# A rebuilt front half of an attention and gMLP block: V and the output projection in 64x128 tiles, weights loaded into both halves, new lists, five half masks and two copies on GpSimd

## The chip, the cores and the metric

The kernel runs on one core of one Trainium2 chip. The metric is device time in microseconds (us). The core has TensorE (PE in the profile, with its weight loads as PEld), VectorE (DVE), ScalarE (ACT), GpSimd (POOL) and SyncE (SP, which here only issues DMAs). Each engine works through its own list in order.

## The reference

Two residual blocks over one sequence of 2048 tokens with 448 features, all inputs in bf16.

```python
S, D, H, Dh, Fh = 2048, 448, 16, 28, 896
# block A: dilated sliding attention, 8 keys at distance 0, 2, ..., 14
qkv = layernorm(x) @ wqkv
logits[s, w] = q[s] . k[s - 2 w] * Dh**-0.5      # masked where s - 2 w < 0
h = x + (softmax(logits) @ v[s - 2 w]) @ wo
# block B: spatial gating
z = gelu(layernorm(h) @ w_in);  z1, z2 = z[:, :Fh], layernorm(z[:, Fh:])
g = w_sp @ z2 + b_sp[:, None]                    # 2048 x 2048 matrix over the tokens
out = h + (z1 * g) @ w_out
```

## The kernel before, in words

The sequence is handled as two halves of 1024 tokens that lie side by side: the features are cut into 7 chunks of 64, and of each chunk the first half's 64 features stand on partitions 0 to 63 and the second half's on 64 to 127 (`xh`). Matmuls with 64 contraction rows then run in pairs, one on each half of the array, into two PSUM banks. For that the weights must be there twice, once in each half of the partitions.

The stages, each named as in the code:

- x is loaded in 16 blocks of 128 tokens (`x0` to `x15`); a unit u is the pair of blocks u and u + 8. Layernorm is statistics (`bn`), aggregate (L819), inverse deviation (`rs`, on GpSimd with L808 and L809, or on ScalarE) and normalization (`nrm`, L838). The result is transposed, for units 0 to 2 of the first layernorm on TensorE (`tT`, L854, then an eviction `ev`), for the others by a DMA transpose on SP's queue (`tD`, L845). The last 16 tokens of the first half are also needed as a halo for the second (`bnh`, `rsh`, `nrmh`, `tTh`, `evh`).
- Q and K (`mmq`, `mmk`, L965) are computed in column chunks, of 128, 128, 256 and 512 tokens of each half, and evicted with L803 (ScalarE) or L805 (VectorE). Their weights are padded from 28 to 32 columns a head, by copies from a staging area (`cpq`, `cpk`).
- Attention runs in 9 tiles of 114 tokens of each half. `mmv` (L1005) makes V for the tile's keys, even and odd tokens apart, in 64x64 tiles of the array: 28 matmuls that read `xh` with a stride of two. `mml` (L1040) makes the logits of all 16 heads, `exp` (L1053) on ScalarE the exponentials, `mask` (L1060) on VectorE multiplies them by a band, `mmr` (L1069) sums them with a matrix of ones, `mmo` (L1089) applies them to V, `ln` and `rex` (L1077, L1099) make the reciprocal of the sums, `ot` (L1107) divides.
- `mmy` (L1143) is the output projection, 8 matmuls of 128x128 a unit: four heads stand on the 128 rows. `h` (L1151) adds x. A second layernorm follows, and z2 (`mmz2`, L1163), Gelu, its layernorm (`bn3`, `rs3`, `nrm3`), z1 (`mmz1`, L1207), the gate (`g`, L1244, 28 groups of 16 matmuls), `ua` and `um` (L1254, L1262), the last projection (`wo0` to `wo15`, L1273), `oa` (L1281) and the store.

The order of the work on each of the five lists is written out by hand in `SEQ`: five tuples of task numbers, for SP, GpSimd, VectorE, ScalarE and TensorE. A task that may run on several engines runs on the one in whose tuple it stands. `replay` walks through the tuples with estimated durations and only hands out buffers with it (PSUM banks, `E`, `V`, `L` and the like); the order itself is the tuples'. Matmuls that only keep TensorE busy can be put in gaps once the task `c_warm` has been placed; before has it at the end of VectorE's tuple, so that there are none.

Of the weights only one copy is loaded, into partitions 0 to 63. wq, wk and wv are loaded on ScalarE's queue (L730). VectorE or ScalarE copies them into the other half: `cpq`, `cpk` (eight copies of 64x1568), `cpv10` (64x3136), `cpw` (four of w_in). The x loads from unit 2 on wait on SP's queue for x8.

## Time and profile before

| | |
|---|---|
| median of 3 runs | 246.23 us (245.85, 246.23, 247.01) |
| span of the profiled execution | 247.4 us, 1.17 above the median of the runs and 0.4 above the slowest |
| TensorE busy | 232.1 us, 94% of the span |
| VectorE, ScalarE, GpSimd busy | 143.3, 91.4, 28.8 us |
| first matmul of Q/K | at 12.38 us |
| first gate matmul of the chain | at 126.57 us |
| last matmul ends | at 244.57 us |

The page lists a time for the profiled execution only as its span, so the span stands for it. A span is counted from the first to the last instruction. The chain of the profile follows the work back from the last instruction: each piece is given with its start, its length and its line; `issue` in it is time for which the profile shows no reason. A matmul's own duration is longer than the time it costs, since matmuls overlap: what a step costs is read from the chain's pieces, not from the mean of its matmuls. PSUM is the matmul's output memory, in eight banks.

### The profile page before, as it was taken

The page shows a single profiled execution, that of the slowest core. Times are in us where ns is not written, and L with a number is a line of the kernel's source. Part 1 is how long each engine was busy: PE and PEld are TensorE (multiplying, and loading weights), DVE is VectorE, ACT ScalarE, POOL GpSimd, SP SyncE. Part 2 cuts the span into 40 slices and gives each one's busy share as a digit, 9 for nine tenths or more (in the row PEclk, how much of TensorE's full clock was granted, in tenths as well). Part 3 has the DMA queues.
Part 4 walks back from the last instruction along what each step waited for, and adds up shares of the span by engine and source line. Part 5 has one row for each costly group of instructions (what it writes and reads, how often), then busy time and mean ns, then how long its engine had stood idle before and what let it go on. Part 6 is the DMA issues. An engine that isn't in the chain of part 4 may idle for free.

```text
span 247.4 us, 6649 instructions
## 1 busy us (share of the span) xinstructions
PE 232.1 (94%) x3004; PEld 123.7 (50%) x3004; DVE 143.3 (58%) x281; ACT 91.4 (37%) x103; POOL 28.8 (12%) x69
## 2 busy tenths in 40 slices
PE   0399799999999999999999999999999999999995
PEld 0297485445556555555544444444444444444442
DVE  6697847779999897798970022335021407541743
ACT  2668784886979965575740000000000000000000
POOL 2843010000021112104530000000000000000000
DMA  6935965893224976886733333100000000010113
GB/s 159 255 80 61 138 91 98 128 154 71 46 40 85 152 197 124 180 147 150 108 85 85 87 85 85 42 3 0 0 0 0 3 0 0 2 46 29 56 57 111
DMA packets 54436, 20.02 MB, mean 81 GB/s; under 512 B 46584, under 2 KB 54280, under 8 KB 54408
## 3 DMA queue, kind: packets, MB, share of 16 engines
q1 hardware_dynamic: 52584, 18.05, 37.4%
q10 hardware_dynamic: 1824, 1.55, 2.8%
q8 instruction: 23, 0.38, 0.7%
q14 instruction: 5, 0.04, 0.1%
HBM read 6.39 MB, written 1.84 MB: 33 GB/s over the span
## 4 chain that ended last, share of the span: by engine, by line
PE 93%; DMA 3%; issue 1%; ACT 1%; ACTq 1%; DVE 0%
PE psum L1244 39%; PE psum L965 11%; PE psum L1163 9%; PE psum L1273 9%; PE psum L1207 9%; PE psum L1005 5%; PE psum L1143 5%; DMA z2p<-in_A_wqkv_dram 3%; PE psum L1040 3%; PE psum L1089 2%; PE psum L1069 1%; ACT reg L803 1%; ACTq L723 1%; ACT xh L803 0%; ACTq L730 0%
## 5 line engine op out<-in xcount | busy, mean ns | idle before, releaser
L1254 DVE TENSOR_TENSOR ub<-psum,reg 128x512 bf16<-128x512 f32 x28 | 18.8, 687 | 64.3 <-PE psum L1244 64.2
L1244 PE MATMUL psum<-reg,z2p 128*128 128x512 bf16 x224 | 50.0, 379 | 0.0
L1244 PE MATMUL psum<-wspT_lo,z2p 128*128 128x512 bf16 x224 | 49.0, 379 | 0.0
L1244 PEld LDWEIGHTS psum<-wspT_lo,z2p 128*128 128x128 bf16 x224 | 21.8, 98 | 26.6 <-issue 0.4
L1244 PEld LDWEIGHTS psum<-reg,z2p 128*128 128x128 bf16 x224 | 21.9, 98 | 26.1
L965 PE MATMUL psum<-xh,reg 64*128 64x128 bf16 (+3 forms) x448 | 28.5, 290 | 2.8 <-issue 2.0
L965 PEld LDWEIGHTS psum<-xh,reg 64*128 64x128 bf16 x448 | 19.4, 105 | 10.5 <-issue 3.4
L1163 PE MATMUL psum<-w_in,xh 64*128 64x448 bf16 x224 | 22.5, 349 | 0.0
L1273 PE MATMUL psum<-reg 128*128 128x448 bf16 x112 | 22.3, 352 | 0.0
L1207 PE MATMUL psum<-xh,w_in 64*128 64x512 bf16 x196 | 22.2, 376 | 0.0
L818 DVE BATCH_NORM_STATS2 st<-x_tm 128x6 f32<-128x448 bf16 x32 | 19.5, 609 | 1.0 <-DMA x_tm<-in_A_x_dram 0.8
L1179 DVE BATCH_NORM_STATS2 st<-z2p 128x6 f32<-128x448 bf16 x32 | 17.7, 612 | 2.6 <-ACT z2p L1173 2.5
L803 ACT ACTIVATE reg<-psum 128x896 bf16<-128x896 f32 (+3 forms) x21 | 16.8, 824 | 5.8 <-PE psum L965 4.2
L1053 ACT ACTIVATE reg<-psum 128x928 bf16<-128x928 f32 x18 | 16.1, 943 | 6.4 <-PE psum L1040 6.4
L1281 DVE TENSOR_TENSOR tring<-psum,x_tm 128x448 bf16<-128x448 f32 x16 | 9.6, 616 | 14.0 <-PE psum L1273 14.0
L808 POOL TENSOR_SCALAR rs<-mv 128x2 f32<-128x2 f32 x21 | 6.3, 300 | 93.7 <-DVE mv L819 78.4
L1173 ACT ACTIVATE z2p<-psum 128x896 bf16<-128x896 f32 x16 | 14.2, 916 | 6.8 <-PE psum L1163 6.8
L1163 PEld LDWEIGHTS psum<-w_in,xh 64*128 64x128 bf16 x224 | 11.9, 94 | 9.5 <-issue 0.9
L1217 ACT ACTIVATE reg<-psum 128x1024 bf16<-128x1024 f32 x14 | 13.7, 1030 | 7.8 <-PE psum L1207 7.8
L1273 PEld LDWEIGHTS psum<-reg 128*128 128x128 bf16 x112 | 11.0, 98 | 10.6
L1207 PEld LDWEIGHTS psum<-xh,w_in 64*128 64x128 bf16 x196 | 11.1, 94 | 9.7
L809 POOL TENSOR_TENSOR rs<-rs,nhalf 128x2 f32<-128x2 f32 x21 | 15.6, 743 | 1.8
(63 smaller groups left out, 201.2 us busy)
## 6 DMA issues: line engine op xcount, KB each, us to landing
out_dram<-tring SPq DMA_DIRECT2D x16, 112.0 KB, 1.7
x_tm<-in_A_x_dram SPq DMA_DIRECT2D x13, 112.0 KB, 5.7
w_in<-in_B_w_in_dram SPq DMA_DIRECT2D x2, 448.0 KB, 5.5
z2p<-in_A_wqkv_dram ACTq DMA_DIRECT2D x2, 392.0 KB, 6.3
reg<-in_B_w_out_dram SPq DMA_DIRECT2D x1, 784.0 KB, 4.8
w_in<-in_B_w_in_dram SPq DMA_DIRECT2D x2, 336.0 KB, 5.1
reg<-in_B_b_sp_dram SPq DMA_DIRECT2D x1, 512.0 KB, 4.2
reg<-in_A_wo_dram SPq DMA_DIRECT2D x4, 98.0 KB
```

What stands on the lines that cost most here:

```text
L803: iss("act", lambda e: e.activation(dst, src, AF.Copy), reads=rd, writes=wr)
L809: iss("pool", lambda e: e.tensor_tensor(dst, dst, nh, ALU.pow), reads=rr + [r_nhalf], writes=rr)
L818: iss("dve", lambda e: e.bn_stats(st[:, b, :], x_tm[:, b, :]), reads=[r_x[b]], writes=[rl[b]])
L965: iss("pe", lambda e, c=c, s=s, gi=gi, lhs=lhs: e.matmul(psum[:, bk[s] * 512 + cw * gi:bk[s] * 512 + cw * gi + cw], lhs, xh[64 * s:64 * s ...
L1053: iss("act", lambda e: e.activation(E[:, es[0], 2 * n:2 * n + 2, :], pair_view(lb, 0, 8 * JW), AF.Exp, scale=SCALE), reads=[r_bank[lb[0]], ...
L1163: iss("pe", lambda e, c=c, s=s: e.matmul(psum[:, zb[s] * 512:zb[s] * 512 + D], xh[64 * s:64 * s + 64, c, HX + 128 * u:HX + 128 * u + 128], ...
L1173: iss("act", lambda e: e.activation(z2p[:, u:u + 9:8, D * k:D * k + D], pair_view(zb, 0, D), AF.Gelu_apprx_tanh), reads=[r_bank[zb[0]], r_ ...
L1179: iss("dve", lambda e, b=b: e.bn_stats(st3[:, b, k, :], z2p[:, b, D * k:D * k + D]), reads=[r_z2[b][k]], writes=[r_st3[b][k]])
L1207: iss("pe", lambda e, c=c, s=s: e.matmul(psum[:, bk[s] * 512:bk[s] * 512 + 512], w_in[64 * s:64 * s + 64, c, 128 * f:128 * f + 128], xh[64 ...
L1244: iss("pe", lambda e, b=b: e.matmul(psum[:, gb[0] * 512:gb[0] * 512 + 512], z2p[:, b, 128 * f:128 * f + 128], src[:, b, 512 * (tc % 2):512 ...
L1254: iss("dve", lambda e: e.tensor_tensor(ub[:, us_[0], :], psum[:, gb[0] * 512:gb[0] * 512 + 512], bb[:, 512 * tc:512 * tc + 512], ALU.add), ...
L1273: iss("pe", lambda e, f=f: e.matmul(psum[:, wb[0] * 512:wb[0] * 512 + D], z1p[f][:, 128 * m:128 * m + 128], w_out[:, f, :], start=(f == 0) ...
```

## The change

It rebuilds the front half and writes all five lists anew. Part by part:

- V: a copy `xv` (one a tile, 128x896) first sorts the even and odd tokens of the tile's keys, on VectorE (tiles 0, 2, 4), ScalarE (1, 5, 6, 8) or GpSimd (3, 7). `mmv` is then 14 matmuls of 64x128 instead of 28 of 64x64.
- Output projection: the heads are laid out so that two stand on each half of 64 rows. `mmo` writes to other rows for that, and `mmy` is 16 matmuls of 64x128 instead of 8 of 128x128; wo is loaded into four row groups, 8 groups of columns each (`wo2`), on SP's queue.
- Weights: wq, wk, wv, wo and w_in are loaded twice, once into each half. The copies `cpv10` and `cpw` are gone; four copies `cpq`, `cpk` of 128x1568 remain for the padding. The first halves of wq, wk and wv are issued on SP's queue, the second on ScalarE's.
- Q/K chunks are 256, 256 and 512 columns (K 256, 270 and 512).
- `mask` is cut into two halves of 128x928, each behind its own `exp`. Five of the 18 are on GpSimd: both of tile 0, the first of tiles 4 and 8, the second of tile 6.
- `mml` reads 28 rows instead of 32; `mmr` is always 8 matmuls; `mmo` no longer waits for `ln`.
- The zeroing of `thalo` and of wo's padding moves from VectorE to GpSimd, and the x loads no longer wait for x8.
- The planner's search code goes; `replay` has other durations and still only hands out buffers and fills gaps. `c_warm` stands in the middle of VectorE's tuple.

The new beginning of each list, by task names: SP: xhalo x1 x0 wq0 x2 x14 x12 x10 x15 wk0 x11 x7 x3 x13 x5 wv0 x6 wo_ld0 x4 wo_ld3 tD1_3 tD1_7 tD1_5 tD1_4 tD1_6 win1_00 wsp0_0. ScalarE: x8 x9 wq1 rs1_1 rs1_0 wk1 wv1 ev1_1 cpq1 xv1 evq0_0 cpk1. VectorE: bnh bn1_1 bn1_9 bn1_8 ag1_1 bn1_0 ag1_0 nrm1_1 nrm1_9 nrm1_0 nrm1_8 nrmh cpq0 ev1_0 bn1_11 bn1_10 evh bn1_12 xv0 cpk0 bn1_13. GpSimd: c_nhalf c_eps c_wpadq rsh c_wpadk c_ident c_V c_th0 c_mband c_wo0 c_xpad rs1_3 c_ones rs1_7 rs1_5 mask0_1 c_kpad rs1_6 mask0_0 xv3 mask4_0 mask6_1 rs2_1 xv7 rs2_0 mask8_0 rs2_2. TensorE: tT1_1 tT1_0 tTh mmq0_0 mmq0_2 mmk0_0 mmk0_2 mmv0 mmv1 tT1_2 mml1 mml0 mmq1_0 mmq1_2 mmk1_1 mmv2 mmk1_3 mmk1_0 mmr1 mmo1_0 mmo0_0 mmr0 mmo1_1 mmo0_1 mmk1_2 mmv3 mmk2_2; later, around tile 4: mml5_0 mml5_1 mml4_0 mml4_1 mmy1 mmo5_0 mmr5 mmo5_1 mml6_0 mml6_1 mmv6 mmr4.

```diff
+CQ = [0, 256, 512, ST]
+CK = [0, 256, 526, ST + HALO]
+XV_ON = ("dve", "act", "pool")
+MASK_ON = ("dve", "pool")
...
-            t_w[p] = dma(eng, "w" + p, lambda e: e.dma_start(
-                w_st[p], A_wqkv[:, c0:c0 + D].rearrange("(c p) n -> p c n", p=64)),
-                D * D * 2, prio=prio, writes=[r_st[p]])
+            t_w[p] = [dma(eng, "w%s%d" % (p, s), lambda e, s=s: e.dma_start(
+                w_ld[p][64 * s:64 * s + 64], A_wqkv[:, c0:c0 + D].rearrange("(c p) n -> p c n", p=64)),
+                D * D * 2, writes=[r_ld[p][s]], issue=0.65, bw=350.0) for s, eng in ((0, "sp"), (1, "act"))]
...
-                copy(tk[0].eng, v(1), v(0), [r_win[z][0][n]], [r_win[z][1][n]])
+                for s in range(2):
+                    t = dma("sp", "win%d_%d%d" % (z, n, s), lambda e, s=s, c0=c0, c1=c1: e.dma_start(
+                        w_in[64 * s:64 * s + 64, c0:c1, FH * z:FH * z + FH],
...
-        for u in range(2, NU):
-            for b in (u, u + 8):
-                t_x[b].deps.append(t_x[8])
-                t_x[b].waits.append(t_x[8])
...
+                copy(tk[0].eng, xv[:, xs[0], :, :].rearrange("p c (w j) -> p c w j", w=2),
+                     xh[:, :, o:o + 128].rearrange("p c (j w) -> p c w j", w=2), rx, [r_xv[xs[0]]])
...
-                    for w in range(2):
-                        for s in range(2):
-                            iss("pe", lambda e, c=c, s=s, w=w: e.matmul(
-                                psum[64 * w:64 * w + 64, bk[s] * 512:bk[s] * 512 + D],
-                                xh[64 * s:64 * s + 64, c, HX - HALO + a + w:HX - HALO + a + w + 127:2],
+                    for s in range(2):
+                        iss("pe", lambda e, c=c, s=s: e.matmul(
+                            psum[:, bk[s] * 512:bk[s] * 512 + D],
+                            xv[64 * s:64 * s + 64, xs[0], c, :],
+                            wv[64 * s:64 * s + 64, c, :], start=(c == 0), stop=(c == NC7 - 1)),
...
-                iss("dve", lambda e: e.tensor_tensor(ev, ev, mk, ALU.mult), reads=r_E[es[0]] + [r_mband], writes=r_E[es[0]])
+                    ev = E[:, es[0], 2 * n:2 * n + 2, :].rearrange("p h (x j) -> p (h x) j", j=JW)
+                    mk = mband[:, :].unsqueeze(1).to_broadcast([128, 16, JW])
+                    iss(tk[0].eng, lambda e: e.tensor_tensor(ev, ev, mk, ALU.mult), reads=[r_E[es[0]][n], r_mband], writes=[r_E[es[0]][n]])
...
-                to = add("mmo%d_%d" % (i, qd), "pe", 0.08, em, deps=[tk, tv, to] + ([tn] if O_AFTER_LN else []), prio=T + OFF["o"] + 0.01 * qd,
+                                    iss("pe", lambda e, w=w, hh=hh, s=s, hp=hp, e_=e_, sg=sg: e.matmul(
+                                        psum[64 * s + 32 * e_:64 * s + 32 * e_ + 32, ob[w] * 512 + hp * JW:ob[w] * 512 + hp * JW + JW],
+                                        V[64 * w:64 * w + 64, vs[0], s, 2 * hp + e_, :],
+                                        E[64 * w:64 * w + 64, es[0], hh, sg * JW:sg * JW + JW],
+                                        tile_position=(64 * w, 64 * s + 32 * e_)),
...
-                for s in range(2):
-                    for g in range(4):
-                        iss("pe", lambda e, s=s, g=g: e.matmul(psum[:, bk[s] * 512:bk[s] * 512 + D],
-                                                              qT[:, s, g, 128 * u:128 * u + 128], wo_p[:, g, :],
-                                                              start=(g == 0), stop=(g == 3)),
+                for x in range(8):
+                    for s in range(2):
+                        iss("pe", lambda e, s=s, x=x: e.matmul(psum[:, bk[s] * 512:bk[s] * 512 + D],
+                                                              oT[64 * s:64 * s + 64, x, 128 * u:128 * u + 128],
+                                                              wo2[64 * s:64 * s + 64, x, :],
+                                                              start=(x == 0), stop=(x == 7)),
```

## The prediction

> **What bounds the kernel now.** I read the shares by engine first, then the chain that ended last (its sum, then its pieces), then windows on single lines, and last the GpSimd rows.
>
> ```profile
> span 247.4 us, 6649 instructions
> ...
> PE 232.1 (94%) x3004; PEld 123.7 (50%) x3004; DVE 143.3 (58%) x281; ACT 91.4 (37%) x103; POOL 28.8 (12%) x69
> ...
> GB/s 159 255 80 61 138 91 98 128 154 71 46 40 85 152 197 124 180 147 150 108 85 85 87 85 85 42 3 0 0 0 0 3 0 0 2 46 29 56 57 111
> ...
> PE 93%; DMA 3%; issue 1%; ACT 1%; ACTq 1%; DVE 0%
> ```
>
> The order of matmuls is the bound: TensorE carries 93% of the chain. Only the head is something else, and one hole of 1.74 us:
>
> ```profile
> 2.92 7.07 DMA z2p<-in_A_wqkv_dram
> ...
> 10.01 1.51 ACT reg L803
> 11.52 0.81 ACT xh L803
> ...
> 12.38 9.04 PE psum L965 x164
> ...
> 28.68 1.74 issue
> ```
>
> So a gain must come from an earlier start than 12.38, from TensorE work that goes away, or from holes. What does TensorE pay for the steps that the change rebuilds? The chain's pieces again:
>
> ```profile
> 76.13 1.47 PE psum L1005 x28
> 77.60 1.62 PE psum L1143 x8
> ...
> 84.88 3.13 PE psum L1143 x16
> ...
> 99.48 1.32 PE psum L1163 x14
> ```
>
> A V tile (L1005, 64x64 tiles) costs 1.45 to 1.47, an output projection (L1143, 128x128) 1.62 alone and 3.13 for two in a row: 2 x 1.62 - 3.13 = 0.11 us is what one change of tile shape costs. The 64x128 form does 14 matmuls of 448 columns in 1.32 (L1163), 94 ns each.
>
> The first Q/K matmuls (L965, 128 columns) run at two speeds. In the windows on that line the columns are TensorE's busy time and matmuls, the weight loads', the granted clock (1.00 in both), and DMA:
>
> ```profile
> 14.38:15.38 1.00, 1.00 (x22) 1.00 (x18) 1.00 0.00 0
> ...
> 18.38:19.38 1.00, 1.00 (x42) 1.00 (x38) 1.00 0.00 0
> ```
>
> 22 a us in the first 5 us of work, 42 after. And GpSimd beside VectorE's copy at 18.89 (0.97 us):
>
> ```profile
> 17.91 0.27 POOL L808 TENSOR_SCALAR rs<-mv 128x2 f32<-128x2 f32 x1 [1.25 <-DVE mv L819]
> ...
> 19.13 0.81 POOL L808 TENSOR_SCALAR rs<-mv 128x2 f32<-128x2 f32 x1 [0.16 <-POOL rs L809]
> ```
>
> Its median is 0.22; beside the copy it took 0.81 and ended 0.08 after it.
>
> **The change, part by part.** The sum is against the profiled execution, span 247.4, which is 1.17 above the median of the three runs (246.23); I take the difference off the median.
>
> *Start.* wq came second on ScalarE's queue (landed 9.99; wk before it 7.70), and then 1.51 of copy into one half. Now each half has its own load, one on SP's queue and one on ScalarE's, right behind the first four x blocks: each stands where wk stood, 7.7. Then VectorE's list decides, from its first data at 3.13: halo statistics 0.78, four statistics at 0.62, two aggregates 0.2, ScalarE's 0.51 for the inverse deviation, four normalizations 0.37, halo 0.49, copy cpq0 0.62 (the 64x1568 row; twice the partitions are taken as free), eviction of the transpose at most 1.09 (the 128x896 CAST): 10.4. The start gains 2.0.
>
> *Q/K chunks of 256 instead of 2 x 128.* Not half the matmul time: 128 columns at 42 a us are 24 ns, 256 are 55.8 (84 in 4.69), so nothing is won warm. Five slow us do 114 x 128 columns, that is 57 of the 112 wide matmuls; 55 x 55.8 ns = 3.1 remain: 8.1 against 9.03. Done at 18.5, not 21.41. The Trainium skill (TensorE: Matmul & The Clock Gate, Part 1) has the slow clock end after some 3.4 us of work. Here the trace has 5; by 3.4 the stretch would take 7.5 (an estimate), and the sum would be 0.6 lower, as far as the next wait lets it.
>
> *V's weights.* V now comes right after Q/K and needs both halves of wv, each behind most of the loads: 14 x blocks of 112 KB and six halves of 392 KB are 4.0 MB. The first two slices of before moved 2.56 MB by 12.4 us; 1.47 MB more at the 255 GB/s of the second slice ends at 18.1. Just hidden. If it is not, every us late is a us.
>
> *Next.* Two V tiles 2.64, the third transpose waits for its normalization: VectorE's list has by then x13 in front (a load of about 15.3 by the same rate) and eight more of its steps, 21.2; then 0.5 and two logit tiles 1.28: 23.0, against 26.36. The second chunk needs unit 3 through the DMA transpose behind nrm1_11 (20.1 by the list; 4.0 to land): 24.1. Of the zeroing, two fills move from VectorE to GpSimd. wo's is the longer, and the load of wo that waits for it on SP's queue has x4 and all five transposes behind it; by GpSimd's rows (0.47, 0.5, 1.59, four selects at 0.23, and at most 2 for the fill) it is done by 12, and the first transpose isn't ready before 20. The wait of the x loads for x8 on SP's queue (2.2 us) goes; x blocks behind wq come no earlier, since the queue is full.
>
> From 24.1: Q 28 x 2 x 55.8 ns = 3.1, K 3.3, V2 and V3 2.64, sums 0.64, attention 1.3: 35.1, the point that before reaches at 39.27: 4.2 ahead. The 512 columns need nrm1_14. VectorE's list up to it: 16 statistics 9.9, 8 aggregates 1.6, 16 normalizations 5.9, halo 1.5, two weight copies 1.2, two transpose evictions and two xv at 0.5 each 2.1, two half masks 1.1, two evictions 1.22 and 1.09, together 25.6; from 3.13, with 2.4 of waits (x13, Q before its eviction): 31.2, plus 4.0 to land is 35.2, no wait worth counting. I keep 4.2.
>
> *Tile shapes.* V and the projection in the 64x128 form are the same columns (14 x 94 ns = 1.32 for V, 16 x 94 = 1.51 for the projection); what goes is the change of shape around them. By the two lists TensorE changes shape 51 times before and 31 after, 6 of the 20 fewer lie before the 39.27 point: 14 x 0.11 = 1.5 us. All on the chain, none of it under other work.
>
> *Copies that go.* Eight Q/K copies, the V copy and four w_in copies leave VectorE (5 x 0.61, 0.97, 2 x 1.09) and ScalarE (3 x 1.51, 2.44, 3.19); four of 0.62 or 1.51, nine xv copies of 896 elements and masks cut in halves come. VectorE's sum to 130 us was 105.5; copies -6.2 + 1.2, zeroing -1.2, masks 10.1 to 13 x 0.56, xv and transposes + 2.6, one Q/K eviction and more -1.5 make some 98. I cost it at nothing: TensorE covers it (10.00 of 10 in every window from 50 us). Without that cover the xv copies would cost 9 x 0.4 to 0.97.
>
> *Loads.* w_in twice is 1.57 MB more, wo 0.39 MB more, on SP's queue, past which the transposes of the second layernorm are moved. Between nothing and 6.3 us (784 KB at 255 GB/s twice, all exposed); I take nothing, because w_in's rows (5.1 to 5.5 us to landing) leave room: z2 first needs it near 75, and on SP's list only transposes of the weights that z2 doesn't use stand between it and the last transpose of x, at 32. bb is issued last of the first-half rows; its first user waits until all eight banks hold a gate, some 20 us into that stage.
>
> *GpSimd.* mask0_0, 0_1, 4_0, 6_1, 8_0 and xv3, xv7. No row of before has such an operation. Lower end: selects 64x58 0.23 and 128x128 0.292 give 0.89 ns an element, so 0.9 us for 928; upper end: three streams at the 0.83 ns an element of ident's fill (0.204, 0.1 of it fixed), with the fixed part 2.4, and once more as long where VectorE has the port. VectorE pays 1.118 for a whole mask, 0.56 for half. Who waits: sums and attention of the tile in TensorE's queue, with everything behind them. For tile 4, TensorE has 5.7 us of other work between its logits and its sum (logits 1.28, projection 1.5, tile 5's sum and attention 0.97, tile 6's logits 0.64, V6 1.32); counted from tile 5's logits, three exponentials of 0.94 come to 3.2, and a mask of 2 (nearer the upper end, since it reads two operands) ends at 5.2: 0.5 in hand. mask0_0 stands behind rs1_6, whose statistics VectorE's list has at 26: done near 29.5, needed at 31.4. mask6_1 also stands ahead of rs2_1 in GpSimd's list, behind which are nrm2_1, its transpose and the first z2. I take half a mask's overrun, 0.25 a piece, 5 x 0.25 = 1.2; ends: -0.5 (VectorE freed of 2.8 at a place that counts) and 12 (five masks uncovered at 2.4).
>
> The Trainium skill (GPSIMD Engine Reference, Elementwise — side-by-side cycle accounting) gives 4497 ns for 2048 elements, estimated 2.0 us for 928; by it the sum would stay as it is.
>
> *Sum.* -4.2 - 1.5 + 1.2 = -4.5; the tail (28 matmuls at L1273, 0.62, store) is the same. 246.23 - 4.5 = 241.7; span 242.9.
>
> **Rivals.** *A, the port (slower).* Beside VectorE's two-input or fast operations GpSimd's masks stop, and VectorE stops for them; the masks then come late for TensorE. For it: the 0.81 row. The price if each of the five comes 2.4 late and the copies 1 each: 12 + 2 - 5.7 = +8.3, so 254.5; it is slower than before once a GpSimd operation delays TensorE by more than 5.7/7 = 0.8 us on average. Against: 0.5 to 2 us of other matmuls in front of each. The Trainium skill, SBUF — State Buffer, Who interferes with whom, has this rule: the pair of ports is locked for a whole instruction, and two SBUF inputs on VectorE are enough; the 0.81 agrees for a copy, no row here has a two-input case.
>
> *B, the doubled loads (no change).* If the loads run at the mean of the first three slices (159, 255 and 80: 165 GB/s), 4.0 MB end at 24.4, V starts 5.9 later than I say, TensorE's list has nothing else to do meanwhile, and only the 1.1 of waiting at 24 comes back: 241.7 + 4.8 = 246.5. For it: the DMA busy digits are 9 in the second slice already. Against: in the third slice of before hardly a load was left to ask for.
>
> *C, covers hold (faster).* No mask late and no wait at 24: 246.23 - 5.7 - 1.1 = 239.4.
>
> **Numbers.** Forecast 0.47, C 0.20, A 0.20, B 0.13. Half a per cent (1.2 us) is about what can be told from no change. Faster by more: 0.45 of the forecast's, C's 0.20, 0.03 of milder A and B, 0.68. Same: 0.11 (half of B, edges of the others). Slower 0.21 (0.17 of A, 0.04 of B). Forecast's own range: 239.5 to 244; the whole, a tenth left out at each end: 238.0 to 249.5, past B and into A.
>
> **What would show it.** Right: first L965 matmul near 10.4; V tiles at 1.32 and projections at 1.51 in the chain; the 39.27 point near 35; TensorE full from 50 us; mask rows on GpSimd under 2.4. Wrong: holes on TensorE before sums that end with GpSimd, VectorE's normalizations stretched beside GpSimd, V waiting for wv beyond 19, z2 waiting for w_in.

## The result: 6.0% slower

The changed kernel takes 261.23 us, the median of four runs (259.45 to 263.10). The kernel before took 246.42 beside it (245.85 to 247.01). The ratio is 1.0599, with an interval of 1.0541 to 1.0657 (ratios and intervals, here and below, compare fast executions alone; medians count all). The prediction said 241.7 and gave "slower" 0.21: the sign is wrong, and 261.23 lies outside its range.

The profiled execution of the changed kernel took 260.51 us with a span of 258.5. In every run that lists both, the time is 1.7 to 2.1 us above the span. So before's profiled execution, with its span of 247.4, took some 249.3 us (an estimate): about 3 above its median, and not 1.17, which holds a span against times. The two spans differ by 11.1 us, the two medians by 14.8; what follows accounts for the 11.1. First the changed kernel's page: span, busy time, granted clock, memory traffic, and the chain's shares by engine.

```profile
span 258.5 us, 6319 instructions
...
PE 234.6 (91%) x2822; PEld 119.2 (46%) x2822; DVE 137.5 (53%) x281; ACT 88.6 (34%) x103; POOL 38.8 (15%) x76
...
PEclk9999999996599999999999999999999999999999
...
GB/s 175 237 242 109 53 83 137 179 211 115 5 3 81 151 145 162 142 171 130 114 171 116 81 81 84 81 42 0 3 0 0 0 0 3 0 18 0 56 91 122
...
PE 74%; DMA 10%; DVE 9%; issue 3%; ACT 2%; SPq 0%; DVEq 0%
```

TensorE carried 93% of the chain before and carries 74% now. The clock row has a 6 and a 5; before's mean clock is 1.000. All four executions of the changed kernel show a mean clock of 0.973 to 0.980. Next the chain's pieces in order of time (start, length, what):

```profile
17.45 3.23 PE psum L759 x56
...
35.47 4.12 DMA xh<-tring
...
39.84 1.70 PE psum L759 x14
...
57.02 0.19 PE psum L838 x8
57.21 3.48 issue
60.69 1.56 PE psum L838 x110
...
86.05 6.42 DMA xh<-tring
...
92.51 2.82 PE psum L972 x28
...
136.73 71.76 PE psum L1049 x332
```

Compare places that hold the same work. Before's pieces there:

```profile
39.27 0.64 PE psum L1040 x61
...
57.07 0.47 PE psum L1089 x47
...
126.57 72.63 PE psum L1244 x336
```

First Q/K matmul: 12.38 before, 10.86 after. Attention of two tiles and V of four done (the prediction's "39.27 point"; in the changed kernel the 512-column chunks of Q/K begin here): 39.27 against 39.84. Attention of four tiles and V of five done: 56.9 against 57.0 (before is at 57.54, of which 0.64 are the logits of one tile more). First gate matmul: 126.57 against 136.73. From there to the end of the span: 120.8 against 121.8. So in these two executions the gain at the start is gone by 40 us, at 57 us the two are level, and some 10 us are lost between 57 us and the gate. One us more goes behind it.

What is lost between: a hole of 3.48 us in the middle of a task of logits, after 8 matmuls, which the profile ends with "issue" and not with an operand; 0.57 more at 64 us; a halved clock behind the hole; and a wait of 2.40 for the first transposes of gMLP (z2, L972). Windows of the changed kernel, columns as before (TensorE, its weight loads, VectorE, ScalarE and GpSimd busy, clock, DMA share, GB/s):

```profile
0.00:57.10 57.10, 43.75 (x986) 27.84 (x987) 38.40 (x74) 38.40 (x48) 16.52 (x40) 1.00 0.82 158
58.00:60.00 2.00, 0.00 (x0) 0.00 (x0) 0.16 (x1) 0.00 (x0) 0.00 (x0) 1.00 0.97 168
60.56:70.80 10.24, 9.41 (x284) 5.18 (x285) 4.45 (x6) 6.80 (x8) 2.46 (x2) 0.50 0.20 43
```

TensorE was busy 9.41 of 10.24 us at half the clock; if all of that work took twice as long, 4.7 us are lost there (an estimate). 3.48 + 0.57 + 4.7 + 2.40 = 11.15; the fewer changes of tile shape give at most 1.5 back. That leaves 9.7, near the 10 that are to be explained.

The hole begins after 986 matmuls. Before had its hole of 1.74 us, which the prediction showed without asking what made it, after 478:

```profile
0.00:28.60 28.60, 18.27 (x478) 15.09 (x478) 21.84 (x53) 18.39 (x25) 11.86 (x35) 1.00 0.72 144
```

986 - 478 = 508 = 4 x 127. The changed kernel's page lists a queue of kind "instruction", with its packets, MB and share:

```profile
q8 instruction: 22, 0.36, 0.6%
```

That is 22 packets of 16 KB for 2822 matmuls: one packet for some 128 matmuls and their weight loads. The queues of the changed kernel (packets, MB, share of 16 engines) from 49.7 to 57.8 us, and then from 57.8 to 59.4:

```profile
q1 hardware_dynamic: 1749, 1.65, 101.4%
```

```profile
q1 hardware_dynamic: 184, 0.27, 109.7%
q8 instruction: 1, 0.02, 5.2%
```

In the first 8.1 us 1.65 MB of data moved and no instruction packet; the next packet (57.85 in the trace) came when TensorE had already run dry. The pause alone doesn't make it late: before has 7.3 us between two packets (49.11 and 56.41) and no hole. TensorE's count does. In the gate stage, where hardly any data moves, packets start after 2364, 2492 and 2619 matmuls. Counted back in steps of 127.5, the packet in question would start after some 836. Two windows:

```profile
0.00:51.40 51.40, 38.05 (x839) 24.74 (x839) 34.79 (x70) 33.70 (x44) 16.52 (x40) 1.00 0.79 152
...
0.00:158.57 158.57, 138.12 (x2364) 74.62 (x2365) 103.67 (x215) 88.58 (x103) 38.83 (x76) 0.97 0.70 128
```

TensorE was there at 51.4 us, and the packet started at 57.85: 6.4 us later (an estimate). Before's packet of 56.41 comes 0.9 us after its count, reckoned in the same way.

The kernel's own code, before and after, has such a count. The planner's `fetch` takes 256 instructions to a packet, has TensorE ask for one 320 instructions (160 matmuls with their weight loads) before it is needed (`CHUNK, ASK, NEED = 256, 115, 435`), and lets it start no earlier than 0.3 us before the last load issued so far lands by its own estimate (`self.landed - 0.3`). The prediction didn't use it.

My theory after this: **a packet of TensorE's instructions came late behind the data loads, TensorE ran dry, and its clock was halved for it.** Rivals: GpSimd (the prediction's own), the doubled bytes as such, and the new lists.

### The profile page after: what moved, and what is told of

Read it like the earlier page. It is cut to its first block, busy times and chain, and to the rows that moved or that the text cites. A ratio compares the mean times of both kernels' runs of the same rounds, so it can differ in the third digit from the quotient of the medians.

```text
span 258.5 us, 6319 instructions
## 1 busy us (share of the span) xinstructions
PE 234.6 (91%) x2822; PEld 119.2 (46%) x2822; DVE 137.5 (53%) x281; ACT 88.6 (34%) x103; POOL 38.8 (15%) x76
## 3 DMA queue, kind: packets, MB, share of 16 engines
q10 hardware_dynamic: 1680, 1.43, 2.4%
## 4 chain that ended last, share of the span: by engine, by line
PE 74%; DMA 10%; DVE 9%; issue 3%; ACT 2%; SPq 0%; DVEq 0%
PE psum L1049 36%; PE psum L1015 8%; PE psum L972 8%; PE psum L759 6%; PE psum L1075 5%; PE psum L807 4%; DMA xh<-tring 4%; DMA z2p<-in_A_wqkv_dram 4%; PE psum L951 3%; DVE tring L641 2%; PE psum L838 2%; DMA out_dram<-tring 1%; DVE reg L860 1%; PE psum L896 1%; DVE tring L1083 1%
## 5 line engine op out<-in xcount | busy, mean ns | idle before, releaser
L1059 DVE TENSOR_TENSOR reg<-psum,reg 128x512 bf16<-128x512 f32 x28 | 18.8, 688 | 77.2 <-PE psum L1049 77.2
L1049 PE MATMUL psum<-reg,z2p 128*128 128x512 bf16 x224 | 49.7, 379 | 0.0
L759 PE MATMUL psum<-xh,reg 64*128 64x256 bf16 (+2 forms) x336 | 28.6, 328 | 4.2 <-DVE xh L605 1.7
L972 PE MATMUL psum<-w_in,xh 64*128 64x448 bf16 x224 | 22.3, 349 | 2.4 <-DMA xh<-tring 2.4
L759 PEld LDWEIGHTS psum<-xh,reg 64*128 64x128 bf16 x336 | 17.2, 102 | 13.8 <-DVE xh L605 1.8
L603 ACT ACTIVATE reg<-psum 128x1024 bf16<-128x1024 f32 (+2 forms) x20 | 18.0, 908 | 9.3 <-PE psum L759 7.5
L617 DVE BATCH_NORM_STATS2 st<-x_tm 128x6 f32<-128x448 bf16 x32 | 18.6, 615 | 3.4 <-DMA x_tm<-in_A_x_dram 3.4
L972 PEld LDWEIGHTS psum<-w_in,xh 64*128 64x128 bf16 x224 | 10.8, 94 | 13.1 <-DMA xh<-tring 2.8
L951 PE MATMUL psum<-reg 64*128 64x448 bf16 x128 | 15.1, 377 | 0.8 <-issue 0.6
L1025 ACT ACTIVATE reg<-psum 128x1024 bf16<-128x1024 f32 x14 | 13.7, 1024 | 5.9 <-PE psum L1015 5.9
L860 POOL TENSOR_TENSOR reg<-reg,mband 128x928 bf16<-128x928 bf16 x5 | 9.3, 1862 | 37.6 <-ACT reg L852 37.3
L641 DVE TENSOR_SCALAR tring<-x_tm,mv,rs 128x448 bf16<-128x448 bf16 x32 | 14.3, 478 | 1.2 <-POOL rs L609 1.1
L807 PE MATMUL psum<-reg,xv 64*128 64x448 bf16 x126 | 14.1, 370 | 0.8 <-DVE xv L605 0.8
```

Of the source, the lines that this page charges most:

```text
L603: iss("act", lambda e: e.activation(dst, src, AF.Copy), reads=rd, writes=wr)
L617: iss("dve", lambda e: e.bn_stats(st[:, b, :], x_tm[:, b, :]), reads=[r_x[b]], writes=[rl[b]])
L641: iss("dve", lambda e: e.tensor_scalar(tring[:, h[0], :].rearrange("p (c s q f) -> p s q c f", c=NC7, s=2, q=2)[:, n], x_tm[:, b, :].rearr ...
L759: iss("pe", lambda e, c=c, s=s, gi=gi, lhs=lhs: e.matmul(psum[:, bk[s] * 512 + cw * gi:bk[s] * 512 + cw * gi + cw], lhs, xh[64 * s:64 * s ...
L807: iss("pe", lambda e, c=c, s=s: e.matmul(psum[:, bk[s] * 512:bk[s] * 512 + D], xv[64 * s:64 * s + 64, xs[0], c, :], wv[64 * s:64 * s + 64, ...
L951: iss("pe", lambda e, s=s, x=x: e.matmul(psum[:, bk[s] * 512:bk[s] * 512 + D], oT[64 * s:64 * s + 64, x, 128 * u:128 * u + 128], wo2[64 * ...
```

## The experiments

All times stand beside runs of the kernel before made along with them. "Holes" are TensorE's idle times at 50 to 90 us that end with nothing the profile shows; "half clock" is where the granted clock fell to 0.5 between its first rise to 1.00 and the store stage; "gate" is the first gate matmul. The last three are from one profiled execution each.

| run | median us | ratio (95%) | holes, largest | half clock | gate |
|---|---|---|---|---|---|
| changed kernel | 261.23 | 1.060 (1.054 to 1.066) | 4.0, 3.5 | 60.6-70.8 | 136.7 |
| e1_spread4 | 261.49 | 1.057 (1.038 to 1.076) | 7.7, 5.5 | 67.4-74.2 | 139.9 |
| e2_spread6 | 261.02 | no interval; 257.46 and 264.58 | 3.9, 1.9 | 60.6-70.8 | 134.7 |
| e3_no_pool | 263.94 | 1.067 (1.063 to 1.071) | 7.5, 6.3 | 61.6-75.2, 95.7-99.1 | 141.2 |
| e4_early_k | 263.25 | 1.064 (1.047 to 1.081) | 4.7, 4.0 | 61.9-68.7, 92.6-96.0 | 137.8 |
| e5_one_by_one | 261.44 | 1.056 (1.049 to 1.063) | 4.0, 1.4 | 90.7-97.5 | 138.8 |
| e6_np_one | 265.57 | 1.073 (1.065 to 1.081) | 7.0, 2.8 | 63.7-67.1, 91.0-97.8 | 140.5 |
| e7_copies | 259.86 | 1.051 (1.044 to 1.058) | 0.8, 0.6 | 60.6-70.9 | 137.6 |
| e8_before_loads | 253.49 | 1.024 (1.017 to 1.031) | 4.9, 4.6 | 59.9-66.7 | 131.6 |
| e9_order | 259.18 | 1.048 (1.041 to 1.054) | 2.8, 1.3 | 60.7-67.5, 98.2-101.6 | 135.4 |
| e10_order_np | 257.54 | 1.042 (1.034 to 1.051) | 4.0, 2.1 | 63.5-66.9 | 133.0 |
| e11_copies_later | 259.97 | 1.050 (1.042 to 1.057) | 2.2, 1.6 | 60.6-70.8 | 136.7 |
| e12_early | 265.32 | 1.070 (1.062 to 1.077) | 4.6, 1.7 | 18.1-21.5, 69.3-72.7, 117.1-120.5 | 143.0 |
| e13_early_np | 262.75 | 1.052 (1.043 to 1.062) | 3.2, 1.0 | 110.2-113.6 | 135.6 |
| e14_before_later | 249.27 | 1.009 (1.005 to 1.012) | 0.4, 0.4 | none | 126.2 |
| e15_gmlp_first | 260.23 | 1.043 (1.031 to 1.055) | 4.9, 2.0 | 61.8-65.2 | 132.2 |
| e16_quiet | 275.11 | 1.102 (1.092 to 1.112) | 5.2, 1.7 | 52.8-56.2, 66.4-69.8, 86.9-90.3 | 135.3 |
| e17_v_between | 255.93 | 1.035 (1.020 to 1.049) | 1.9, 1.3 | none | 131.0 |

In the diffs the lists show the task names in place of their numbers.

### First: is it GpSimd, or where the loads stand?

Four late halves of w_in behind two of w_sp's loads (e1), six of them (e2):

```diff
 SP: ... wo2 wo1
-    win1_10 win1_11 win0_10 win0_11 wsp0_9 wsp0_2 tD2_1 ...
+    wsp0_9 wsp0_2 win1_10 win1_11 win0_10 win0_11 tD2_1 ...          # e1
+    wsp0_9 wsp0_2 win1_10 win1_11 win0_00 win0_01 win0_10 win0_11 tD2_1 ...  # e2
```

> The changed kernel with one thing moved: win1_10, win1_11, win0_10 and win0_11, four loads of 336 KB that SP issues between 48.9 and 51.5 us, stand behind wsp0_2 on SP's list, where the trace has the data queues idle (62 to 78 us). Theory (TensorE's own instructions are fetched through the same DMA engines and come late behind these loads; the hole of 3.48 us at 57.21 then throttles the clock to 0.5 for 10 us): no hole near 57, granted clock 1.00 from 60 to 70, 3.5 + 4.9 us less, about 252. Rival 1 (GpSimd's masks are what holds TensorE, the hole included): nothing changes, 259 to 263. Rival 2 (the hole is a wait for the data of the logits): nothing changes either.

> As the one before, and win0_00 and win0_01 (448 KB each, issued at 84.9 and 93.4 between the transposes of the second layernorm) stand there too, at about 62 us. Theory: the transpose that the second z2 waited for (2.4 us, landed 6.4 after its issue) lands in some 3 us as in the kernel before, and another 2 to 3 us go: about 250. Rival (that transpose is late because VectorE's list is late): no more than the one before.

Both missed: the hole didn't go, it moved, to 60.05 and 64.88 us in e1 and 59.77 and 65.08 in e2. In both runs TensorE had then done 1113 and 1241 matmuls: 986 plus 127 and plus 255. The loads still fell into the same stretch, since w_sp's two were done sooner (SP issues the late halves from 58.4 us on in e1). The part that e2 adds did what was expected of it: z2's first wait is 0.4 us in place of 2.8 in e1, and the gate begins 5.2 us sooner.

Without GpSimd's masks and copies:

```diff
-GpSimd: ... mask0_1 ... mask0_0 xv3 mask4_0 mask6_1 ... xv7 ... mask8_0 ...
+VectorE: ... ag1_6 mask0_1 ... evq1_2 mask0_0 ... evv2 xv3 ... (the others beside their other halves)
```

> The changed kernel with the five half masks and the two xv copies on VectorE instead of GpSimd, nothing else moved. Theory: normalizations no longer stretch beside GpSimd (1.9 and 2.5 us for two and three in the trace), which gives some 3 us back before 36 us and costs VectorE 2 x 0.64 + 1.07 there; the hole at 57 and the slow clock stay: 258 to 262. Rival 1 (GpSimd is the cause of the loss): 250 or less.

This refutes GpSimd as the main cause: with none of it the time is no shorter, and the hole is longer (6.29 us, after 1114 matmuls). But GpSimd does cost something earlier. The changed kernel's masks on GpSimd, and VectorE's normalizations beside them:

```profile
27.13 1.97 POOL L860 TENSOR_TENSOR reg<-reg,mband 128x928 bf16<-128x928 bf16 x1 [2.70 <-ACT reg L852]
...
30.91 1.80 POOL L860 TENSOR_TENSOR reg<-reg,mband 128x928 bf16<-128x928 bf16 x1
```

```profile
27.64 1.89 DVE L641 TENSOR_SCALAR tring<-x_tm,mv,rs 128x448 bf16<-128x448 bf16 x2
...
31.59 2.55 DVE L641 TENSOR_SCALAR tring<-x_tm,mv,rs 128x448 bf16<-128x448 bf16 x3
```

The same groups without GpSimd (their line is L642 there):

```profile
28.54 0.69 DVE L642 TENSOR_SCALAR tring<-x_tm,mv,rs 128x448 bf16<-128x448 bf16 x2
...
31.83 1.00 DVE L642 TENSOR_SCALAR tring<-x_tm,mv,rs 128x448 bf16<-128x448 bf16 x3
```

Five normalizations take 1.69 us alone and 4.44 beside the masks. The 512-column point comes at 38.28 without GpSimd, 1.5 us sooner than in the changed kernel.

K's weights earlier, each half right behind wq's:

```diff
-SP: ... wq0 x2 x14 x12 x10 x15 wk0 ...    ScalarE: x8 x9 wq1 rs1_1 rs1_0 wk1 ...
+SP: ... wq0 wk0 x2 x14 x12 x10 x15 ...    ScalarE: x8 x9 wq1 wk1 rs1_1 rs1_0 ...
```

> The changed kernel with wk0 right behind wq0 on SP's queue and wk1 right behind wq1 on ScalarE's, ahead of the x blocks and of ScalarE's inverse deviations. Theory (wk1 was issued at 6.76 and landed at 16.67): K's first matmul at 15 to 16.7 instead of 17.45; of that at most 1 us is left at 40 us, because VectorE's list decides when the last transpose is issued: 259 to 262. Rival (the doubled early loads are the whole loss): 250 or less.

No gain. K's first matmul comes at 18.39, since VectorE's list has statistics of x11 (now later) ahead of K's weight copy. The holes are at 58.00 and 61.15 us, after 986 and 1113 matmuls.

### Second: do late packets make the hole?

The converse first (e8): the kernel before, with nothing changed but w_in's second halves loaded in place of copied, in a bunch where the changed kernel has them.

```diff
-copy(tk[0].eng, v(1), v(0), ...)                     # cpw1_0, cpw1_1, cpw0_0, cpw0_1
+dma("sp", ..., e.dma_start(v(1), B_w_in[...]), ...)
 SP: ... wo1
+    cpw1_1 cpw1_0
     win0_0
+    cpw0_0
     wsp0_2 ...
```

> The kernel before, with the second halves of w_in loaded instead of copied, both halves of three pieces standing together on SP behind the last load of wo, as in the changed kernel; no other part of the change. 'Instructions behind data': a hole of 2 to 6 us at about 55 to 62 us, on a multiple of 127 to 128 matmuls from 478, and the clock at 0.5 behind it: 251 to 256 us. Rival 'the bytes are harmless, the hole belongs to the new lists': no hole; 244 to 247, the four copies being gone from ScalarE and VectorE.

As the first theory said. Windows of that run (the first ends where the hole begins) and the chain's piece:

```profile
0.00:56.80 56.80, 46.47 (x1241) 31.37 (x1242) 42.59 (x77) 37.82 (x48) 12.74 (x37) 1.00 0.78 142
...
58.00:60.00 2.00, 0.00 (x0) 0.00 (x0) 1.72 (x5) 0.00 (x0) 0.00 (x0) 0.96 1.91 128
60.00:62.00 2.00, 0.63 (x57) 0.62 (x58) 0.00 (x0) 0.00 (x0) 0.00 (x0) 0.50 0.14 25
```

```profile
56.73 4.64 issue
```

The same loads make the same hole, at one of the same counts, with the same half clock, in a kernel without GpSimd's masks, the new tiles or the new lists: 2.4%, 6.0 us. In its trace the instruction packets come at 46.53 and then at 58.62.

Next the changed kernel with six waits more, so that only one load of wo or w_in is in flight (e5):

```diff
+chain([wo2, wo1, win1_10, win1_11, win0_10, win0_11], first=win1_01)   # each waits for the landing of the one before
```

> The changed kernel; the third and fourth of wo's loads and the next four halves of w_in are issued only when the one before has landed (six waits on SP, nothing else). In the four runs so far TensorE stopped each time after 986, 1113 or 1241 matmuls, 127 or 128 apart, and the 16 KB packet of the instruction queue that came next stood behind the w_in loads. Theory 'instructions behind data': with at most one load of 448 KB in flight no packet waits over 2 us, the hole of 3.5 us shrinks below 1 and the granted clock stays at 1.00 after it (4.9 us less), so 252 to 254 us. Rival 'another cause of the hole' (the w_in bytes themselves, the transposes, a data wait): a hole of 2 to 6 us stays, 259 to 264.

Half right. The clock is at 1.00 from 57 to 90 us and no hole is over 1.4. The time is the same. What came instead is on SP's queue (start, length) and in TensorE's waits (total, times, longest):

```profile
80.40 5.69 SPq L933 DMA_TRANSPOSE wspT_lo<-in_B_w_sp_dram  x2
86.13 0.61 SPq L556 DMA_DIRECT2D w_in<-in_B_w_in_dram  x1
86.79 1.31 SPq L649 DMA_TRANSPOSE xh<-tring  x1
```

```profile
PE psum L973 <- DMA xh<-tring: 4.8, 1, 4.8
```

w_sp's loads wait for each other on SP, a gMLP transpose stands behind them, and TensorE waits 4.8 us for it. The clock was halved from 90.7 to 97.5.

The same with all six late pieces in the chain and no GpSimd (e6):

```diff
+chain([wo2, wo1, win1_10, win1_11, win0_10, win0_11, win0_00, win0_01], first=win1_01)
 (and the lists of e3)
```

> As the run with loads one by one, with all six late halves of w_in in that chain (the two of the lower chunk behind the others) and the five masks and two copies of GpSimd on VectorE. 'Instructions behind data': no hole, no slow clock, no wait of 2.4 us for the first gMLP transpose, and the 1.5 us that the run without GpSimd was ahead at 57 us: 248 to 250. Rival 'another cause': the hole stays, 258 to 264. If GpSimd only ever cost what a late VectorE list cost, it comes out as the run one by one less 2 us for the transpose.

Worse: w_in's chain holds SP from 56.6 to 78.6 us, so everything behind is later (z2 waits 5.3), and TensorE still has holes of 7.0 us, the largest of 2.8 at 83 us.

With fewer bytes: VectorE copies the second halves, at two places (e7, e11).

```diff
-dma("sp", "win%d_%d1", ...)
+add("win%d_%d1", "dve", 1.1, tensor_copy(v(1), v(0)))
 VectorE: ... ot3 win1_01 win1_11 ...        # e7; in e11 win1_11 stands behind nrm2_1
```

> One part of the change undone: four halves of w_in are loaded and the other four are copied from them by VectorE (1.09 us each, as before), the first two in the stretch up to 60 us and two near 90; all else as changed. 'Instructions behind data': 1.57 MB less to load, 0.78 of it around 50 us: the hole shrinks below 1.5 and the clock stays whole or nearly, 252 to 255 us with the copies. Rival 'GpSimd, the tiles or the projection': hole and half clock stay, 260 to 265.

> The run in which VectorE copies the second halves, with the second copy behind nrm2_1 (about 75 us), so that VectorE doesn't stand waiting for its load as it did at 52 to 57.4 us (that emptied TensorE by 3.8 us). Nothing else differs from the changed kernel but the 1.57 MB. 'Instructions behind data': the largest hole between 55 and 76 us is under 1.5 us, the clock at 1.00 there: 252 to 256. Rival 'the hole belongs to the lists, not to the bytes': a hole of 2 to 6 us and 7 to 10 us of half clock, 259 to 263.

e7 is a poor test: the copy of win1_11 waited on VectorE for its load until 57.4, and TensorE waited 3.8 us for VectorE. The half clock of 10.2 us came all the same: here it follows a wait for VectorE and not a late packet. e11 has the fewer bytes and still has holes of up to 1.6 us and 10.2 us of half clock: wo's last two, two pieces of w_in in place of four, and two of w_sp are issued from 47.3 on, as close together as in the changed kernel, and instruction packets come at 45.48 and then only at 55.63. About two thirds of that bunch (1.6 of 2.3 MB) still go with holes and half clock, so the doubled bytes alone are not the cause. But TensorE also waited 1.1 us for VectorE right ahead of them (at 56.4), so the run doesn't give the share of either.

And the kernel before once more: its first w_in load moved from 24 us to behind the layernorm's last transpose (e14).

```diff
 SP: ... wo3
-    win1_0
     tD1_4 tD1_7 tD1_6 tD1_5
+    win1_0
     wsp0_0 ...
```

> The kernel before with its first w_in load (448 KB, issued at 24 us) behind the last transpose of the layer norm (36.5 us). That kernel has a hole of 1.7 us at 28.7 us, after 478 matmuls, and its packet of 27.61 us stood behind that load. 'Instructions behind data' holds for the kernel before as well: the hole goes, 1 to 1.8 us faster, 244.9 to 246. Rival: the x loads held the packet, not w_in: 246 to 247.5.

The hole of 28.68 is gone, as expected, but the time, expected at 244.9 to 246, is 249.27 (1.009). There are three new holes in its chain, 2.2 us together. Whether before has the hole of 28.68 in every execution isn't known; its profiled one was some 3 us above the median.

```profile
36.36 0.77 issue
...
41.46 0.71 issue
...
46.90 0.74 issue
```

### Third: what stays when the loads are mended?

SP's order mended in the run with loads one by one: w_sp's loads alternate with w_in's, and none of them stands between the first two gMLP transposes (e9); then GpSimd's three early items on VectorE as well (e10).

```diff
 SP: ... wo2 wo1 win1_10
-    win1_11 win0_10 win0_11 wsp0_9 wsp0_2 tD2_1 wsp0_10 wsp0_3 win0_00 tD2_0 wsp0_11 tD2_2 win0_01
+    wsp0_9 win1_11 wsp0_2 win0_10 wsp0_10 win0_11 wsp0_3 tD2_1 tD2_0 win0_00 tD2_2 wsp0_11 win0_01
+VectorE: ... ag1_6 mask0_1 ... evq1_2 mask0_0 ... evv2 xv3 ...       # e10 only
```

> As the run with loads one by one, with SP's order mended: that run kept the clock at 1.00 from 57 to 90 us and had no hole above 1.4 us, but its first gMLP transpose (tD2_0) stood on SP behind two waiting loads of w_sp until 86.8 us, landed at 91.8, and the clock was halved then. Here w_sp's loads alternate with w_in's, nothing waits in front of tD2_1 and tD2_0, and win0_00 stands behind tD2_0. Theory 'instructions behind data, then transposes behind loads': gMLP's wait of 4.8 us and the half clock at 91 us (3.4 us) go: 252 to 256 us. Rival 'VectorE's list sets the start of gMLP' (the normalization for tD2_0 stands behind the last masks): tD2_0 issued at 85 to 86 us all the same, 257 to 260.

> The run with SP's order mended, and of GpSimd's seven items the three early ones (mask0_1, mask0_0, xv3) on VectorE; the four late ones stay on GpSimd. 'GpSimd stretches VectorE's normalizations at 27 to 33 us': the stretch up to 57 us is 1.5 us shorter, as it was without GpSimd: 1 to 2 us under the run beside it, 250 to 254. Rival 'what is won up to 57 us is given back at the start of gMLP, which VectorE's list sets': within 0.7 us of the run beside it.

259.18 and 257.54: less gain than the theory said, but the first gate matmul is at 135.4 and 133.0. The 1.6 us between the two fit the 1.5 that GpSimd cost in the early stretch, though their intervals overlap. Holes of 1.3 to 2.1 us stay at the packet counts.

The upper pieces of w_in early, where packets have time to be late (e12), with the early items on VectorE (e13), and with all gMLP transposes ahead of w_sp's later loads (e15):

```diff
 SP: ... tD1_6 win1_00
-    wsp0_0 wsp0_8 win1_01 wsp0_1 wo2 wo1 win1_10 win1_11 win0_10 win0_11 wsp0_9 wsp0_2 tD2_1 ...
+    win1_01 win1_10 win1_11 wo2 wo1 wsp0_0 wsp0_8 wsp0_1 wsp0_9 wsp0_2 tD2_1 win0_10 win0_11 tD2_0 win0_00 win0_01 tD2_2 ...
+    ... w_out tD2_4 tD2_7 tD2_6 wsp0_11 wsp0_4 ...                   # e15; there also VectorE: nrm2_14 bn3_1_1 bn3_0_1
```

> The changed kernel with SP's order alone changed, no wait added: the upper four pieces of w_in and wo's last two stand in one go behind the last transpose of the layer norm (36.7 to about 48 us), w_sp's loads one at a time behind them, and the four lower pieces behind tD2_1 (78 us) and tD2_0 (85 us). The packets of TensorE's instructions that come in 36 to 50 us were used 4 to 8 us after they came, so they have time to wait; those of 51 to 66 us had 3 us or none. Theory 'a late packet hurts only where small matmuls use packets up at 4 us each': the hole at 57 us under 1 us, clock at 1.00 at 57 to 76 us: 250 to 254 us. Rival 'w_sp's loads or the dense matmuls alone hold packets up': holes of 1 to 3 us and a half clock stay, 255 to 260.

> The run with the upper pieces early, and GpSimd's three early items on VectorE. If GpSimd costs what the stretch up to 57 us showed (1.5 us) and nothing gives it back: 1 to 2 us under the run beside it. If the start of gMLP gives it back: the same within 0.7.

> The run with the upper pieces early and GpSimd's three early items on VectorE; in its profile the clock was whole from 14.7 to 110 us, but gMLP's tiles waited from 102.3 to 109.3 us, since two transposes stood on SP until 106.1 behind two waiting loads of w_sp, and the clock was halved then. Here all transposes of the second layer norm stand before w_sp's later loads, and VectorE's first two statistics of the third norm stand behind the last normalization of the second. Theory 'the rest of the loss is transposes behind loads': 4 to 6 us under the run it comes from (its profiled time 258.8, its median 262.8): 253 to 257. Rival 'gMLP waits for VectorE in any order': 258 to 263.

Three misses in time (e13 is 2.6 us under e12, where 1 to 2 were expected, and still at 262.75). The clock is whole from 21.5 to 69 us in e12 and up to 110 in e13, and no hole is over 1.7, but the loss reappears where transposes stand behind waiting loads. e12 was also 2.2 us late at its first V tile: TensorE had waited 2.25 us for VectorE, the clock was 0.5 from 18.1 to 21.5, and 56 Q/K matmuls took 4.78 in place of 3.23. Why it lost its clock there isn't known; e4 and e15 waited 2.6 and 2.4 us at the same place and kept it. In e13, SP and the chain:

```profile
99.44 6.64 SPq L933 DMA_TRANSPOSE wspT_lo<-in_B_w_sp_dram  x2
106.12 2.64 SPq L649 DMA_TRANSPOSE xh<-tring  x2
```

```profile
106.12 3.09 DMA xh<-tring
...
109.26 7.15 PE psum L973 x56
```

e15 takes that wait away: z2 waits 0.8 us in place of 2.9 and the clock is whole from 65 us on. But TensorE has holes of 2.0 and 1.7, and then the gate waits for w_sp's loads, which it put back. The interval (1.031 to 1.055) doesn't tell it from e13 or e10.

Last, are the lists to blame where no load is? In e16 SP issues no load from 52 us to tD2_1:

```diff
 SP: ... wo2 wo1 wsp0_0 wsp0_8
-    wsp0_1 wsp0_9 wsp0_2
     tD2_1 win0_10 win0_11
+    wsp0_1
     tD2_0 ... (the rest of w_sp one after the other behind them)
```

> As the run beside it, with only two of w_sp's loads before tD2_1, so that no load at all runs from about 50 to 70 us. Theory 'every packet behind any load is late': the pieces of 1.0 to 1.5 us by which TensorE stood between 57 and 70 us in the run with the upper pieces early (5.0 us in all) go as well: 3 to 5 us under the run beside it, 249 to 254. Rival 'the new lists' small matmuls outrun the packets by themselves': the same pieces stay, within 1 us of the run beside it; a wait of the gating unit for w_sp behind 126 us would add to either.

Its time says only that the gate then waits for w_sp and for the bias behind it (the warning of its expectation). Its trace says more; it is that of the longest of its four executions, 277.21 us, and by the mean clock (0.98 there, 0.993 and 0.994 in the others) not all of its three halvings are in each. All DMA from 55 to 76 us, a digit for each 0.53 us, and then the packets:

```profile
DMA  0000000001000000010000000100000000001000
...
DMA packets 4, 0.07 MB, mean 3 GB/s; under 512 B 0, under 2 KB 0, under 8 KB 0
...
q8 instruction: 4, 0.07, 1.2%
```

```profile
61.69 0.60 issue
...
64.72 1.56 issue
```

Four instruction packets and nothing else, 4 to 6 us apart, and TensorE still runs dry twice, 2.2 us, after 1114 and 1242 matmuls. e15 has a like case: it stands 1.73 us from 60.17 on, and no data moved from 60 to 62 us, though 139 GB/s did in the 2 us before. So the last rival, the new lists, has a part: they put logits and attention of 58 columns (96 matmuls in 0.96 to 1.00 us) in a row.

The counts say why. With packets starting as in the gate stage, TensorE has some 150 matmuls left when one starts (986 and twelve steps of 127.5 make 2516, against 2364). From the start of a packet to TensorE's going on e16 took 2.3 us both times (60.01 to 62.29, 63.96 to 66.29), and 150 matmuls of 58 columns last 1.6 (estimates). So where only such matmuls follow each other, a hole comes with no load about. The loads add to it: e16's two packets started 2.7 and 3.4 us after their counts, the changed kernel's 6.4, and that hole is 3.48 us in place of 0.60 and 1.56.

e17 is e10 with one task moved on TensorE, nothing else:

```diff
 TensorE: ... mmv5 mml5_0 mml5_1
+    mmv6
     mml4_0 mml4_1 mmy1 mmo5_0 mmr5 mmo5_1 mml6_0 mml6_1
-    mmv6
     mmr4 ...
```

> The run with SP's order mended and GpSimd's early items on VectorE (257.5 us, 1.0423 of the kernel before), with one task moved on TensorE: the 14 matmuls of 448 columns of the next V tile (mmv6, 1.4 us) stand between the two pairs of logits tasks of 58-column matmuls at 57 us, not 300 matmuls behind them. In the run whose memory queues were empty from 55 to 76 us TensorE still stood 0.6 and 1.6 us at the packet counts there. Theory 'the lists put more small matmuls in a row than packets come for': the holes of 57 to 64 us, 3.3 us in the run it comes from, shrink by 1 to 1.4, and the ratio comes to 1.035 to 1.040. Rival 'only loads make holes': the same holes, 1.042 or more; that the moved tile waits for its copy would show as a wait for xv.

The best of the rebuilt kernels, 255.93 us, ratio 1.035. In its profile the clock isn't halved at all (the mean clock of its other executions is 0.993, 0.993 and 0.979), and one hole over a us is left of those from 57 to 64:

```profile
PEclk9999999999999999999999999999999999999999
```

```profile
57.39 1.34 issue
...
79.77 4.83 DMA xh<-tring
...
89.10 5.81 DMA xh<-tring
```

Its interval (1.020 to 1.049) overlaps that of e10, so the gain in time is not shown beyond doubt; the shorter holes are, in one profile each (1.9 us against 4.0). It still starts the gate 4.4 us after the kernel before: TensorE waits 2.6 us for transposes of z2's input, 0.9 for one of Q's, and 2.1 for VectorE and ScalarE at 61 to 80 us. None of these runs beats the kernel before: with no halved clock in its profile and the holes at 1.9, e17 is still 8.2 us above the 247.75 beside it. So all mends together win back some 6 of the 14.8 us; where the rest goes is read from the traces only.

## Why the prediction was wrong, step by step

The spans give the sum: 242.9 forecast, 258.5 measured, 15.6 more. Of these, 4.8 lie ahead of the 39.27 point (4.2 ahead forecast, 0.6 behind measured), 9.9 between it and the gate (0.3 less forecast, 9.6 more measured) and 1.0 behind.

- **Loads, "I take nothing". This is the step that failed.** It asked only whether w_in is there when z2 needs it; it is, z2 never waited for w_in. The loads cost by a way that the step didn't have: TensorE's own instructions come as DMA packets too, beside the loads. Put alone into the kernel before, the bunch costs 6.0 us; in the changed kernel the hole and the half clock are 3.48 + 4.7 = 8.2, of which the new order of small matmuls has a part. The bound of 6.3 was for an exposed load, not for this. A row that pointed at it was in the prediction's first reading, before's hole of 1.74 us in the middle of a task; its matmul count and the memory traffic beside it were not read, nor the planner's `fetch`.
- **"TensorE covers it" (copies at nothing, from 10.00 of 10 in every window).** Cover was read from the list before, and the change wrote new lists. TensorE waits for VectorE's first steps, for transposes behind SP's loads (2.4 us for z2) and for instructions. The new order of small matmuls makes 2.2 us of holes with no load about (e16, one execution).
- **Start, 10.4.** It came at 10.86: a gain of 1.5, not 2.0, and perhaps less, since e8 and e14, whose edits lie behind the start, begin at 11.50 and 11.79 and not at 12.38. wq's halves landed at 8.65 and 8.94, not 7.7, and VectorE waited 0.8 us for them. The copy cpq0 took 1.32 us, priced at 0.62; it ran beside a fill of 1.59 on GpSimd. The eviction took 0.60 of the 1.09 allowed.
- **Q/K's first chunk done at 18.5.** It was 20.68. The wide matmuls cost what was said when warm (57.7 ns each against 55.8), but K waited 0.77 for wk's second half, which landed at 16.67 and was not in the sum, and the slow clock held to 16.2. V's weights landed at 20.63, forecast at 18.1: they were hidden, but only because Q/K was late. Two V and two logits tiles ended at 25.2, not 23.0.
- **39.27 point at 35.1.** It was 39.84; the step lost its whole 4.2. nrm1_14 ran at 35.06, not 31.2. The list's durations were those without GpSimd beside them: five normalizations took 4.44 us in place of 1.69 (2.75 more). The xv copy was mis-sized at 0.5; it took 1.07, with GpSimd beside it or without (1.08 in e3). e3 got 1.5 us back.
- **GpSimd's masks, 1.2.** The price of one was right (1.86 us on the mean against 2), and TensorE hardly waited for masks (0.4 us for a sum). Who paid was VectorE, in the early list. Rival A had the mechanism (the ports) but not the place; it is not what makes the kernel slower, as e3 shows. The Trainium skill (SBUF — State Buffer, Who interferes with whom) says that such fast single-input operations on VectorE and GpSimd's reads lock each other out; the trace agrees, with 0.35 (e3) against 0.95 us a normalization at the first pair.
- **Tile shapes.** V tiles at 1.32 and projections at 1.51 in the chain, as said; one shape change still costs 0.11 (two V tiles 2.75, one 1.43).
- **The tail, "the same".** 1.0 us longer from the gate on. The chain has a store there (240.40, 3.77) that a buffer waited for; what makes the us was not tried.
- **Rivals B and C.** B's delay of V by loads didn't show, but it was near: with Q/K done at 18.5, V would have waited 2.1 us for its weights. C's premise, no mask late, nearly held, and didn't help.

## What to carry to other kernels

Count TensorE's instructions as traffic: find the instruction queue in the profile, divide the matmuls by its packets, and compare idle times that end with "issue" with multiples of that count. Then ask how long the last 150 matmuls ahead of such a point last, against some 2.3 us that a packet takes. Spread loads, and put those that many small matmuls run beside at another place, one or two in flight; but a list that waits for loads holds up the transposes behind it, and two mends here (e5, e13) gave back what they gained that way. A list written for one set of durations has little slack for another: cover must be read from the new order, not from the old windows.

## What the runs showed of the hardware

- TensorE's instructions come in packets of 16 KB, one for 128 matmuls with their weight loads. In the changed kernel and in the runs made from it, the mid-task holes of 50 to 70 us begin after 859, 986, 1113 or 1241 matmuls, within two; before's lies at 478. A packet itself takes 0.9 to 2.0 us; with no data about, the next started 4 us after it while TensorE had small matmuls (e16). Packets start some 150 matmuls before TensorE would run dry in the gate stage (2364 against 2516).
- A packet can come late beside queued data: the changed kernel's of 57.85 started 6.4 us after its count (an estimate), while 1.35 MB moved, and while loads issued before that count were still landing (the last at 61.02). The Trainium skill (DMA: Bandwidth & Descriptors, Queues, rings and completion order) has each engine take turns between its queues, packet by packet. By that rule alone the packet would have waited for a few data packets; a wait like this one doesn't look like it. What holds it longer was not found, and no trace shows when it was asked for.
- After an idle time the clock was halved for 3.4, 6.8, 10.2 or 13.7 us, multiples of 3.41. The Trainium skill (TensorE: Matmul & The Clock Gate, Part 1) has windows of 3.4 us, idle ones halving the clock and busy ones freeing it. The lengths agree. But in e10 holes of 1.25 and 2.10 us with 2.4 us of work between them were enough (the clock was 0.5 from 63.5 to 66.9), and no 3.4 us ahead of it were idle throughout.
- A fill on GpSimd, which only writes, ran beside a copy on VectorE that took 1.32 us in place of 0.63.
